# More loads in flight and a new order of all instructions: a recurrent-attention and gated-MLP kernel on one Trainium2 core

## The chip, the cores and the metric

The kernel runs on one core of a Trainium2 chip. The metric is the device time of one execution in microseconds (us), lower is better. A core has five engines that each follow their own instruction queue in order: TensorE (PE, matmuls), VectorE (DVE), ScalarE (ACT), GpSimd (POOL) and SyncE (SP, which here only issues DMAs). They wait for one another and for DMAs by semaphores.

## What is computed

Four arrays q, k, v, alpha of shape (4 batches, 8 heads, 768 steps, 48) go through a gated linear recurrence, and the 3072 x 384 result goes through a two-layer MLP with a smooth gate:

```python
for t in range(S):
    state = alpha[:, :, t, :, None] * state + k_t (outer) v_t      # per batch and head, 48 x 48
    y[:, :, t] = q_t @ state
x = y as (3072 tokens, 384)
h = x @ w_in                                    # 384 -> 2048
g = h * tanh(log1p(exp(h)))
out = g @ w_out                                 # 2048 -> 384, float32
```

The two weights arrive as 64-bit floats and are turned on the chip into a high and a low part of a narrower float each, so that three matmul passes (high x high, high x low, low x high) keep float32 accuracy.

## The kernel before, in words

**Attention.** The 768 steps are cut into 12 pieces of 64, the 4 batches into 2 pairs: 24 chunks, numbered so that chunk n belongs to pair n % 2 and piece n // 2. A chunk loads one tile `qka` (q, k and alpha, 772 KB; chunk 0 in three parts, chunk 1 in two) and one tile `v` (192 KB). DVE makes the running products of alpha by two scans (`scan_rest` L672, `scan_front` L685) and multiplies k and q by them (L681, L695). PE transposes k ("turn", L724), forms the front half (`from_state` L745/L752 and the scores L763), DVE masks the scores (L778, and L583 for chunks taken in pairs), PE forms the back half (L783/L790) and the state's update (L802), and ACT and DVE write the result as a high and a low part into the tile `xs` (ACT `upper` L831, DVE `lower` L837). The state is then added by DVE (L874) or, where the sum was made on PE (L809), copied by ACT (L872). From chunk `PAIR_FROM` = 8 on, two chunks go together.

Four settings say how a chunk does parts of this. In `DIRECT` (chunks below 8 only) PE writes the last two heads straight to their place by extra small matmuls (L745, L783); a chunk not in it writes them to a side tile `x3`, and six small DMAs of 16 KB (`move`, L858), issued by SP or, where `MOVER` says so, by ACT, carry them into `xs`. In `X_PE` PE subtracts the high part in PSUM (`off`, L844) and ACT copies what is left (L852), in place of DVE's `lower`; the state's update then comes after that as a task of its own. In `STATE_PE` PE adds the old state by two more matmuls (L809) and ACT copies the sum, in place of DVE's L874.

**Weights.** There are 16 blocks f. Each is loaded as 64-bit words (768 KB, L415) into one of two `stage` buffers, DVE puts together its bits in three steps (L428, L433, L438), ACT writes the high part (L449), and the low part is the difference, which `W_LOW` gives to DVE (L455), to POOL in two halves (L477), or to PE in two halves (L467, L468, in a named PSUM bank) with an ACT copy after each (L471). A second load of every block from L491 on serves a range check.

**MLP.** A unit is one weight block f on 2 or 4 chunks: nine matmuls into `h_at` ("up", L1017), four ACT steps, one DVE step (L1044), one ACT step (L1051), one DVE step (L1054), and three matmuls for each chunk into `sums_at` ("down", L1089). `SEGMENTS` sets the order of the 100 units: blocks 0 to 3 on chunks 0 and 1, then on chunks 2 and 3; blocks 4 to 10 on chunks 0 to 3; blocks 0 to 9 on chunks 4 to 7; the other blocks on these; then all 16 blocks on chunks 8 to 11, 12 to 15, 16 to 19 and 20 to 23.

**Order.** The order of the instructions on all engines is made at build time by `Plan.order`, a list planner: each task has an engine, a cost, a latency, a key (a due time in units, from `LEAD`, `DUE_SHIFT`, `W_LEAD`, `W_SHIFT`, `Q_LEAD`, `V_LEAD`, `FIRST_W`), needs and buffers; an engine takes the task that can begin earliest, with a penalty `PER_KEY` for each unit of key beyond its first open task. Buffers are 3 for `qka`, 2 for `v`, 2 for `stage`, 2 for `x3`. Before bulk work is there PE gets fills, matmuls whose results are not used (L1165), to keep it running. The planner holds a clock for loads: a load begins `DMA_FIRST` after its issue or when the load before it is through, and takes its size over `DMA_RATE`. A load may be issued only when the loads in flight and itself are within `FLIGHT` kilobytes; the planner sets the load that it has to wait for (`paced`), and this becomes a real wait on SP's queue:

```python
            if t.size:
                room = FLIGHT - t.size
                for x in reversed(loads):
                    room -= x.size
                    if room < 0:
                        at, t.paced = max(at, x.begin + x.late + 0.1), x
                        break
```

SP issues in order, so whatever stands behind a waiting load waits too.

Of the kernel before, what the change touches and what calls it, by code (L numbers as in the profile page):

```python
# [39 lines left out]
QKA = 2 * NSEG * L + NSEG * (L + 1) + 1  # L40
# [10 lines left out]
    "h": 2, "t": 3, "g": 2, "osb": 8,  # L51
}
LAG = 3
LEAD = 5.5
SPREAD = 3.0
W_LEAD = 4.25
GATE = -2.0
Q_LEAD = 4.75
V_LEAD = 9.75
FIRST_W = -22.25  # L60
CHECK_FROM = 105
CHECK_STEP = 2.0
FILLS = 150
# [7 lines left out]
}  # L71
W_SHIFT = {
    0: -30.0, 1: -2.75, 2: -3.75, 3: -1.75, 4: -3.5, 5: -9.25, 6: 0.25, 7: -4.75, 8: 2.5, 9: 2.75,
    10: 2.25, 11: 7.0, 12: -6.25, 13: -7.75, 14: 30.25, 15: -1.75,
}
X_PE = {0, 1}
SIDES = 2
STATE_PE = {2, 6}
PAIR_FROM = 8
BACK_AFTER = 0.8  # L80
DIRECT = {0, 1, 2, 3, 6, 7}
W_LOW = {
    0: ('PE', 'o0'), 1: ('PE', 'o0'), 2: ('PE', 'o3'), 3: ('PE', 'o3'), 4: ('POOL', ''), 5: ('PE', 'o0'),
    6: ('DVE', ''), 7: ('POOL', ''), 8: ('POOL', ''), 9: ('DVE', ''), 10: ('DVE', ''), 11: ('POOL', ''),
    12: ('POOL', ''), 13: ('POOL', ''), 14: ('DVE', ''), 15: ('POOL', ''),
}
MOVER = {
    (1, 1, 0): 'ACT', (1, 2, 0): 'ACT', (1, 2, 64): 'ACT', (2, 1, 0): 'ACT', (2, 2, 64): 'ACT',
    (3, 0, 64): 'ACT', (3, 1, 64): 'ACT', (3, 2, 64): 'ACT', (4, 0, 0): 'ACT', (5, 1, 0): 'ACT',
    (6, 0, 0): 'ACT', (6, 0, 64): 'ACT', (6, 2, 64): 'ACT', (8, 0, 0): 'ACT', (8, 1, 64): 'ACT',  # L90
}
IN_BANK = 0

STOP_AT = 1e9
LOAD_MARGIN = 1.0
LANES = 8
FLIGHT = 1800.0
BLOCK, BLOCK_USED, FETCH_FIRST, FETCH_LAST = 256, 63, 0.8, 2.5
DMA_RATE, DMA_FIRST, DMA_LAST = 285.0, 1.1, 0.9
ENGINES = ("PE", "DVE", "ACT", "POOL", "SP")  # L100
BEGIN = {"PE": 3.0, "DVE": 4.3, "ACT": 2.2, "POOL": 4.2, "SP": 1.2}

# [19 lines left out]
class Plan:  # L122
# [150 lines left out]


KEYS = 60.0
PER_KEY = {'PE': 0.03, 'DVE': 0.02, 'ACT': 0.02, 'POOL': 0.02, 'SP': 0}


COST = {
    "load": (0.45, 2.0), "apart": (0.19, 0.32),  # L280
    "move": (0.63, 2.5), "store": (0.4, 3.0),
    "fill": (0.23, 0.28), "fill0": (0.44, 0.47),
    "off": (0.55, 0.75), "w off": (0.84, 1.08), "lead": (0.47, 0.58), "bits": (0.87, 0.98),
    "w hi": (0.745, 0.88), "w left": (0.42, 0.56), "w lo": (1.05, 1.2), "w lo2": (0.88, 1.0),
    "w check": (0.92, 1.2),
    "scan": (1.16, 1.27), "inverse": (0.09, 0.21), "mult": (0.6, 0.72), "check": (0.2, 0.34),
    "state": (0.48, 0.55), "state0": (0.5, 0.6), "mask": (0.65, 0.8),
    "front": (1.19, 1.32), "front d": (1.59, 1.72), "front0": (0.76, 0.9), "turn": (0.34, 0.6), "turn2": (0.7, 0.95),
    "front2": (2.09, 2.22), "back2": (1.91, 2.04), "back2 last": (1.18, 1.3), "spread": (0.4, 0.4),
    "turned": (0.46, 0.6), "back": (1.14, 1.26), "back1": (0.75, 0.9), "update": (0.7, 0.85),  # L290
    "state on": (0.42, 0.42),
    "x3 hi": (0.16, 0.3), "x3 lo": (0.2, 0.32), "x hi": (0.39, 0.53), "x lo": (0.48, 0.59),
# [17 lines left out]
def fast_path(ctx, tc, qka, v, w, out, good):  # L310
# [65 lines left out]
    add, last_col = plan.add, NSEG * (L + 1)  # L376
# [221 lines left out]
    def chunk(n):  # L598
        nonlocal last_front, v_apart_read, st_apart_read
        b, c = chunks[n]  # L600
        first, last = c == 0, c == NCH - 1
        paired = n >= PAIR_FROM
        st = state[b]
        key = 0.5 * (due[n // 2 * 2] + due[n // 2 * 2 + 1]) + 0.05 * (n % 2) if paired else due[n]
# [858 lines left out]
```

## Time and profile before

| what | us |
|---|---|
| median of 3 runs | 499.11 (498.87 to 499.72) |
| the profiled execution, its own time | 497.71 |
| its span, from the first to the last instruction | 496.0 |
| PE busy | 484.6 (98% of the span) |
| DVE busy | 323.1 (65%) |
| ACT busy | 382.1 (77%) |
| POOL busy | 25.3 (5%) |

The granted TensorE clock is 0.998 over the span, so all durations are at the upper of its two levels, 2.4 GHz. PE's busy time contains the fills. Matmuls are pipelined and their recorded times overlap, so what a burst costs PE is read as the distance from its start to the start of the next burst.

### The profile page before, as it was taken

The page shows a single profiled execution, that of the slowest core. Times are in us where ns is not written, and L with a number is a line of the kernel's source. Part 1 is how long each engine was busy: PE and PEld are TensorE (multiplying, and loading weights), DVE is VectorE, ACT ScalarE, POOL GpSimd, SP SyncE. Part 2 cuts the span into 40 slices and gives each one's busy share as a digit, 9 for nine tenths or more (in the row PEclk, how much of TensorE's full clock was granted, in tenths as well). Part 3 has the DMA queues.
Part 4 walks back from the last instruction along what each step waited for, and adds up shares of the span by engine and source line. Part 5 has one row for each costly group of instructions (what it writes and reads, how often), then busy time and mean ns, then how long its engine had stood idle before and what let it go on. Part 6 is the DMA issues. An engine that isn't in the chain of part 4 may idle for free.

```text
span 496.0 us, 12822 instructions
## 1 busy us (share of the span) xinstructions
PE 484.6 (98%) x5319; PEld 432.5 (87%) x5319; DVE 323.1 (65%) x522; ACT 382.1 (77%) x864; POOL 25.3 (5%) x27
## 2 busy tenths in 40 slices
PE   6999999999999999999999999999999999999995
PEld 4688889899899989999989899999989899999994
DVE  7999999999973694447867783863474343343333
ACT  3578786886788778857777897889789899997772
POOL 2003201413000000000000000000000000000000
PEclk9999999999999999999999999999999999999999
DMA  7877544606000250115152543603153412100001
GB/s 248 316 285 236 181 151 157 238 35 214 13 0 9 78 172 1 66 59 175 28 213 75 183 164 99 207 24 118 71 171 93 172 41 106 64 1 0 1 0 68
DMA packets 18926, 56.22 MB, mean 113 GB/s; under 512 B 3440, under 2 KB 11312, under 8 KB 18864
## 3 DMA queue, kind: packets, MB, share of 16 engines
q1 hardware_dynamic: 18592, 55.11, 32.5%
q8 instruction: 42, 0.69, 0.6%
q10 hardware_dynamic: 272, 0.26, 0.2%
q14 instruction: 20, 0.16, 0.1%
HBM read 48.87 MB, written 4.72 MB: 108 GB/s over the span
## 4 chain that ended last, share of the span: by engine, by line
PE 85%; DVE 9%; DMA 3%; issue 1%; ACT 1%; SPq 0%; DVEq 0%; ACTq 0%
PE sums_at L1089 39%; PE h_at L1017 37%; PE att_at L790 2%; PE att_at L752 2%; DVE w_lead L433 2%; PE h_at L763 2%; DMA ws<-in_wp_dram 1%; DVE w_lead L438 1%; PE att_at L724 1%; DMA qka<-in_qka_dram 1%; PE h_at L802 1%; DVE w_lead L428 1%; DVE t L1044 1%; DVE g L1054 1%; DVE rest L672 1%
## 5 line engine op out<-in xcount | busy, mean ns | idle before, releaser
L1089 PE MATMUL sums_at<-ws,g 128*128 128x384 f32 x1152 | 223.9, 340 | 0.1
L1017 PE MATMUL h_at<-xs,ws 128*128 128x512 f32 (+1 forms) x900 | 214.2, 384 | 0.2 <-DVE t L1044 0.2
L1089 PEld LDWEIGHTS sums_at<-ws,g 128*128 128x128 f32 x1152 | 202.4, 188 | 8.1 <-ACT ws L471 0.4
L1017 PEld LDWEIGHTS h_at<-xs,ws 128*128 128x128 f32 x900 | 163.3, 188 | 28.4 <-DVE t L1044 0.5
L1054 DVE SCALAR_TENSOR_TENSOR g<-t,g 128x512 fp32r<-128x512 f32 (+1 forms) x100 | 67.8, 679 | 124.2 <-ACT g L1051 123.9
L1026 ACT ACTIVATE t<-h_at 128x512 f32<-128x512 f32 (+1 forms) x100 | 58.0, 580 | 63.6 <-PE h_at L1017 60.8
L1051 ACT ACTIVATE g<-t 128x512 fp32r<-128x512 f32 (+1 forms) x100 | 60.3, 604 | 11.5 <-PE sums_at L1089 5.3
L1029 ACT ACTIVATE t<-t 128x512 f32<-128x512 f32 (+1 forms) x100 | 61.3, 613 | 2.3
L1032 ACT ACTIVATE t<-t 128x512 f32<-128x512 f32 (+1 forms) x100 | 61.2, 612 | 2.2
L1044 DVE SCALAR_TENSOR_TENSOR t<-t,h_at 128x512 f32<-128x512 f32 (+1 forms) x87 | 57.1, 657 | 8.3 <-ACT t L1035 8.2
L1035 ACT ACTIVATE t<-t 128x512 f32<-128x512 f32 (+1 forms) x100 | 60.4, 604 | 0.5
L672 DVE TENSOR_TENSOR_SCAN rest<-qka,behind 112x520 f32<-112x520 f32 x24 | 30.4, 1268 | 0.4 <-DMA qka<-in_qka_dram 0.2
L685 DVE TENSOR_TENSOR_SCAN qka<-qka,ahead 112x520 f32<-112x520 f32 x24 | 30.6, 1274 | 0.0
L477 POOL TENSOR_TENSOR ws<-w_lead,ws 128x384 fp32r<-128x384 f32 x14 | 22.1, 1598 | 98.3 <-ACT ws L449 98.3
L1026 ACT ACTIVATION_READ_ACCUMULATOR t<-h_at 128x1 f32 x100 | 19.4, 194 | 0.0
L1041 DVE COPY held<-h_at 128x512 f32<-128x512 f32 x13 | 9.0, 691 | 15.8 <-ACT t L1026 15.8
L831 ACT ACTIVATE xs<-att_at 112x384 fp32r<-112x384 f32 (+1 forms) x24 | 12.2, 513 | 6.2 <-PE att_at L809 3.4
L695 DVE TENSOR_TENSOR qka<-qka 112x512 f32<-112x512 f32 x24 | 16.4, 684 | 0.1
L681 DVE TENSOR_TENSOR qka<-qka,rest 112x512 f32<-112x512 f32 x24 | 15.8, 659 | 0.0
L433 DVE SCALAR_TENSOR_TENSOR w_lead<-ws,w_lead 128x768 int32<-128x768 int32 x16 | 15.7, 982 | 0.1
L438 DVE SCALAR_TENSOR_TENSOR w_lead<-ws,w_lead 128x768 int32<-128x768 int32 x16 | 15.3, 957 | 0.1
L449 ACT ACTIVATE ws<-w_lead 128x768 fp32r<-128x768 f32 x16 | 13.4, 839 | 2.3 <-DVE w_lead L438 2.2
(100 smaller groups left out, 366.7 us busy)
## 6 DMA issues: line engine op xcount, KB each, us to landing
qka<-in_qka_dram SPq DMA_DIRECT2D x22, 772.5 KB, 5.8
ws<-in_wp_dram SPq DMA_DIRECT2D x16, 768.0 KB, 4.5
wc<-in_wp_dram SPq DMA_DIRECT2D x16, 768.0 KB, 4.5
v<-in_vp_dram SPq DMA_DIRECT2D x24, 192.0 KB, 4.5
out_dram<-osb SPq DMA_DIRECT2D x15, 192.0 KB, 2.6
xs<-x SPq DMA_DIRECT2D x104, 16.0 KB, 1.8
out_dram<-part SPq DMA_DIRECT2D x8, 192.0 KB, 2.6
qka<-in_qka_dram SPq DMA_DIRECT2D x2, 260.5 KB, 4.4
```

Source lines behind the costliest of these rows:

```text
L433: nc.vector.scalar_tensor_tensor(lead.tile, words(1), -0x40000000, lead.tile, ALU.bitwise_and, ALU.bitwise_or)
L672: nc.vector.tensor_tensor_scan(t[:, :0:-1], alpha()[:, :0:-1], behind[:, ::-1], 0.0, ALU.mult, ALU.max)
L685: nc.vector.tensor_tensor_scan(a, a, ahead, 0.0, ALU.mult, ALU.max)
L1017: nc.tensor.matmul(p[:, :N].rearrange("p (c t) -> p c t", c=nt), wi[:, z, f, s], x[:, :, s, a], start=m == 0, stop=m == len(passes) - 1,)
L1026: nc.scalar.activation(wide(t), wide(h), AF.Exp, accum_out=vchk[:, at : at + 1])
L1029: nc.scalar.activation(wide(t), wide(t), AF.Square, bias=1.0)
L1032: nc.scalar.activation(wide(t), wide(t), AF.Ln, bias=0.2, scale=0.2)
L1035: nc.scalar.activation(wide(t), wide(t), AF.Exp, scale=-1.0)
L1044: nc.vector.scalar_tensor_tensor(wide(y), wide(t), 2.5, wide(held), ALU.subtract, ALU.mult)
L1051: nc.scalar.activation(g.tile[:, 0, :N], wide(y), AF.Copy, scale=-0.4, accum_out=own)
L1054: nc.vector.scalar_tensor_tensor(g.tile[:, 1, :N], wide(y), -0.4, g.tile[:, 0, :N].bitcast(F32), ALU.mult, ALU.subtract,)
L1089: nc.tensor.matmul(o.tile, g.tile[:, a, j * C : (j + 1) * C], wo[:, z, f], start=begins and m == 0, stop=end and m == 2,)
```

## The change

It raises `FLIGHT` from 1800 to 3500 KB, gives the planner's loads a higher rate (345 for 285), a longer lead-in (1.7 for 1.1 us) and a shorter end (0.6 for 0.9), writes the loads' sizes larger (791 for 692, 263 for 230), and sets the keys and the choices per chunk and block anew, from which the planner makes another order of all instructions. In the choices, chunks 2 and 4 join `X_PE`, chunks 3 and 4 join `STATE_PE` (2 and 6 stay), chunks 0 and 7 leave `DIRECT`; block 3's low part goes from PE to POOL, those of blocks 6, 9 and 14 from DVE to POOL, and those of blocks 8, 11 and 12 from POOL to DVE. No loop, no tile size and no buffer count changes.

```diff
-LEAD = 5.5
+LEAD = 5.75
-W_LEAD = 4.25
+W_LEAD = 5.5
-Q_LEAD = 4.75
-V_LEAD = 9.75
-FIRST_W = -22.25
+Q_LEAD = 4.0
+V_LEAD = 11.5
+FIRST_W = -18.0
 DUE_SHIFT = {
-    0: -3.75, 1: 1.75, 2: 2.5, 3: 1.0, 4: -1.5, 5: 2.0, 6: 2.0, 7: 2.0, 8: -4.5, 9: -6.5, 10: -11.25,
+    0: 2.25, 1: 2.75, 3: -1.5, 4: -1.0, 5: 0.5, 6: -0.75, 7: 1.5, 8: -3.5, 9: -3.5, 10: -14.75,
...
 W_SHIFT = {
-    0: -30.0, 1: -2.75, 2: -3.75, 3: -1.75, 4: -3.5, 5: -9.25, 6: 0.25, 7: -4.75, 8: 2.5, 9: 2.75,
-    10: 2.25, 11: 7.0, 12: -6.25, 13: -7.75, 14: 30.25, 15: -1.75,
+    0: -21.5, 1: -2.0, 2: -1.75, 3: 0.25, 4: -3.25, 5: -8.5, 6: -1.5, 7: -0.75, 8: 2.25, 9: 3.5, 10: 4.5,
+    12: -7.25, 13: 10.25, 14: 26.5, 15: -2.25,
 }
-X_PE = {0, 1}
+X_PE = {0, 1, 2, 4}
-STATE_PE = {2, 6}
+STATE_PE = {2, 3, 4, 6}
-BACK_AFTER = 0.8
-DIRECT = {0, 1, 2, 3, 6, 7}
+BACK_AFTER = 0.25
+DIRECT = {1, 2, 3, 6}
 W_LOW = {
-    0: ('PE', 'o0'), 1: ('PE', 'o0'), 2: ('PE', 'o3'), 3: ('PE', 'o3'), 4: ('POOL', ''), 5: ('PE', 'o0'),
-    6: ('DVE', ''), 7: ('POOL', ''), 8: ('POOL', ''), 9: ('DVE', ''), 10: ('DVE', ''), 11: ('POOL', ''),
-    12: ('POOL', ''), 13: ('POOL', ''), 14: ('DVE', ''), 15: ('POOL', ''),
+    0: ('PE', 'h'), 1: ('PE', 'o2'), 2: ('PE', 'o3'), 3: ('POOL', ''), 4: ('POOL', ''), 5: ('PE', 'o0'),
+    6: ('POOL', ''), 7: ('POOL', ''), 8: ('DVE', ''), 9: ('POOL', ''), 10: ('DVE', ''), 11: ('DVE', ''),
+    12: ('DVE', ''), 13: ('POOL', ''), 14: ('POOL', ''), 15: ('POOL', ''),
 }
 MOVER = {
-    (1, 1, 0): 'ACT', (1, 2, 0): 'ACT', (1, 2, 64): 'ACT', (2, 1, 0): 'ACT', (2, 2, 64): 'ACT',
...
+    (0, 0, 64): 'ACT', (0, 1, 64): 'ACT', (0, 2, 0): 'ACT', (0, 2, 64): 'ACT', (1, 1, 0): 'ACT',
...
-FLIGHT = 1800.0
+FLIGHT = 3500.0
-DMA_RATE, DMA_FIRST, DMA_LAST = 285.0, 1.1, 0.9
+DMA_RATE, DMA_FIRST, DMA_LAST = 345.0, 1.7, 0.6
-PER_KEY = {'PE': 0.03, 'DVE': 0.02, 'ACT': 0.02, 'POOL': 0.02, 'SP': 0}
+PER_KEY = {'PE': 0.01, 'DVE': 0.02, 'ACT': 0.02, 'POOL': 0, 'SP': 0.12}
-                for z, e, early in ((230, (a_at, QKA), 1.0), (460, (0, a_at), 0.0))
+                for z, e, early in ((267, (a_at, QKA), 1.0), (524, (0, a_at), 0.0))
-                "SP", *COST["load"], key - Q_LEAD, load, uses=[q_buf], size=692
+                "SP", *COST["load"], key - Q_LEAD, load, uses=[q_buf], size=791
```

## Rows read from the trace of the kernel before

**Rows 1.** The page, busy time of each engine (share of the span), instructions.
```profile
PE 484.6 (98%) x5319; PEld 432.5 (87%) x5319; DVE 323.1 (65%) x522; ACT 382.1 (77%) x864; POOL 25.3 (5%) x27
```
**Rows 2.** Stretches: us, busy PE, PEld, DVE, ACT, POOL (instructions), clock, DMA share, GB/s.
```profile
10.00:20.00 10.00, 8.85 (x167) 6.35 (x170) 9.68 (x15) 4.88 (x13) 0.00 (x0) 1.00 0.90 319
...
80.00:100.00 20.00, 19.77 (x246) 17.17 (x245) 19.87 (x28) 16.48 (x35) 6.94 (x4) 1.00 0.57 204
100.00:150.00 50.00, 50.00 (x493) 45.32 (x492) 43.91 (x63) 38.33 (x83) 5.01 (x5) 1.00 0.17 59
```
**Rows 3.** PE in order of time: start, us, line, count [idle before and releaser].
```profile
2.85 3.24 PE L1165 MATMUL sums_at<-minus_ident 128*128 128x512 f32 x7 [2.85 <-ACT minus_ident L336]
...
19.57 0.58 PE L783 MATMUL att_at<-probs,v_apart 64*64 64x64 f32 x24
...
22.34 0.60 PE L724 MATMUL att_at<-ident,qka 112*128 112x112 f32 x4
22.72 1.31 PE L1017 MATMUL h_at<-xs,ws 128*128 128x256 f32 x9
...
33.19 0.70 PE L1165 MATMUL sums_at<-minus_ident 128*128 128x512 f32 x2
```
**Rows 4.** Groups and waits of PE: the fills' group, then its last wait but the tail.
```profile
L1165 PE MATMUL sums_at<-minus_ident 128*128 128x512 f32 x31 | 10.5, 466 | 2.8 <-ACT minus_ident L336 2.8
PE h_at L1017 <- DVE t L1044: 0.2, 1, 0.2
```
**Rows 5.** DVE in order of time, 8 to 19 us.
```profile
8.73 0.56 DVE L428 TENSOR_SCALAR w_lead<-ws 128x768 int32<-128x768 int32 x1 [1.12 <-DMA ws<-in_wp_dram]
...
15.24 1.24 DVE L672 TENSOR_TENSOR_SCAN rest<-qka,behind 112x520 f32<-112x520 f32 x1 [0.25 <-DMA qka<-in_qka_dram]
16.40 0.67 DVE L695 TENSOR_TENSOR qka<-qka 112x512 f32<-112x512 f32 x1
...
17.66 1.23 DVE L685 TENSOR_TENSOR_SCAN qka<-qka,ahead 112x520 f32<-112x520 f32 x1
18.81 0.71 DVE L778 COPY_PREDICATED probs<-causal,att_at 128x512 f32<-128x512 uint32 x1
```
**Rows 6.** Waits of SP's DMA queue for loads: us in total, times, longest.
```profile
SPq L415 <- DMA qka<-in_qka_dram: 10.1, 6, 3.5
SPq L646 <- DMA ws<-in_wp_dram: 4.1, 1, 4.1
```
**Rows 7.** One stretch of 1 us in the head; columns as in the stretches above.
```profile
9.00:10.00 1.00, 0.66 (x33) 0.64 (x33) 0.96 (x2) 0.27 (x1) 0.00 (x0) 1.00 0.59 173
```
**Rows 8.** PE in order of time: bursts that the edits add or take away.
```profile
24.77 0.58 PE L745 MATMUL att_at<-qka,v_apart 48*64 48x64 f32 x24
25.17 0.52 PE L752 MATMUL att_at<-qka,state 48*48 48x64 f32 x24
25.51 0.65 PE L763 MATMUL att_at<-qka 48*64 48x64 f32 x32
26.09 0.91 PE L467 MATMUL sums_at<-w_lead,ident 128*128 128x384 f32 x2
...
27.01 0.81 PE L467 MATMUL sums_at<-w_lead,ident 128*128 128x384 f32 x2
...
75.07 0.90 PE L809 MATMUL att_at<-state,ident 112*112 112x192 f32 x4
75.68 2.36 PE L1017 MATMUL h_at<-xs,ws 128*128 128x512 f32 x9
```
**Rows 9.** DVE in order of time: steps that move, and a scan beside POOL.
```profile
31.65 0.55 DVE L837 TENSOR_TENSOR xs<-att_at,xs 128x384 fp32r<-128x384 f32 x1
...
42.66 0.55 DVE L874 TENSOR_TENSOR state<-att_at,state 112x384 f32<-112x384 f32 x1
...
92.12 2.08 DVE L672 TENSOR_TENSOR_SCAN rest<-qka,behind 112x520 f32<-112x520 f32 x1
```
**Rows 10.** The moves into `xs` up to 110 us: from issue to landing.
```profile
DMA to landing us min/median/max: 1.7/2.4/4.6
```

More of the change, by code (lines that the diff above doesn't have):

```diff
@@ L67 @@
 DUE_SHIFT = {
[3 rows of a table removed]
[3 rows of a table added]
 }
 W_SHIFT = {
-    0: -30.0, 1: -2.75, 2: -3.75, 3: -1.75, 4: -3.5, 5: -9.25, 6: 0.25, 7: -4.75, 8: 2.5, 9: 2.75,
-    10: 2.25, 11: 7.0, 12: -6.25, 13: -7.75, 14: 30.25, 15: -1.75,
+    0: -21.5, 1: -2.0, 2: -1.75, 3: 0.25, 4: -3.25, 5: -8.5, 6: -1.5, 7: -0.75, 8: 2.25, 9: 3.5, 10: 4.5,
+    12: -7.25, 13: 10.25, 14: 26.5, 15: -2.25,
 }
-X_PE = {0, 1}
+X_PE = {0, 1, 2, 4}
 SIDES = 2
-STATE_PE = {2, 6}
+STATE_PE = {2, 3, 4, 6}
 PAIR_FROM = 8
-BACK_AFTER = 0.8
-DIRECT = {0, 1, 2, 3, 6, 7}
+BACK_AFTER = 0.25
+DIRECT = {1, 2, 3, 6}
 W_LOW = {
-    0: ('PE', 'o0'), 1: ('PE', 'o0'), 2: ('PE', 'o3'), 3: ('PE', 'o3'), 4: ('POOL', ''), 5: ('PE', 'o0'),
-    6: ('DVE', ''), 7: ('POOL', ''), 8: ('POOL', ''), 9: ('DVE', ''), 10: ('DVE', ''), 11: ('POOL', ''),
-    12: ('POOL', ''), 13: ('POOL', ''), 14: ('DVE', ''), 15: ('POOL', ''),
+    0: ('PE', 'h'), 1: ('PE', 'o2'), 2: ('PE', 'o3'), 3: ('POOL', ''), 4: ('POOL', ''), 5: ('PE', 'o0'),
+    6: ('POOL', ''), 7: ('POOL', ''), 8: ('DVE', ''), 9: ('POOL', ''), 10: ('DVE', ''), 11: ('DVE', ''),
+    12: ('DVE', ''), 13: ('POOL', ''), 14: ('POOL', ''), 15: ('POOL', ''),
 }
 MOVER = {
-    (1, 1, 0): 'ACT', (1, 2, 0): 'ACT', (1, 2, 64): 'ACT', (2, 1, 0): 'ACT', (2, 2, 64): 'ACT',
-    (3, 0, 64): 'ACT', (3, 1, 64): 'ACT', (3, 2, 64): 'ACT', (4, 0, 0): 'ACT', (5, 1, 0): 'ACT',
-    (6, 0, 0): 'ACT', (6, 0, 64): 'ACT', (6, 2, 64): 'ACT', (8, 0, 0): 'ACT', (8, 1, 64): 'ACT',
+    (0, 0, 64): 'ACT', (0, 1, 64): 'ACT', (0, 2, 0): 'ACT', (0, 2, 64): 'ACT', (1, 1, 0): 'ACT',
+    (1, 2, 64): 'ACT', (2, 2, 0): 'ACT', (4, 2, 64): 'ACT', (5, 2, 64): 'ACT', (6, 0, 0): 'ACT',
+    (7, 0, 64): 'ACT', (7, 1, 64): 'ACT', (7, 2, 64): 'ACT', (8, 2, 64): 'ACT', (9, 2, 64): 'ACT',
 }
@@ L288 @@
     "front": (1.19, 1.32), "front d": (1.59, 1.72), "front0": (0.76, 0.9), "turn": (0.34, 0.6), "turn2": (0.7, 0.95),
-    "front2": (2.09, 2.22), "back2": (1.91, 2.04), "back2 last": (1.18, 1.3), "spread": (0.4, 0.4),
+    "front2": (2.107, 2.24), "back2": (1.903, 2.04), "back2 last": (1.18, 1.3), "spread": (0.4, 0.4),
     "turned": (0.46, 0.6), "back": (1.14, 1.26), "back1": (0.75, 0.9), "update": (0.7, 0.85),
@@ L654, in chunk @@
             got_a, got_k, got_q = (
-                add("SP", *COST["load"], -99 + 0.1 * i, load_part(*e), uses=[q_buf], size=230)
+                add("SP", *COST["load"], -99 + 0.1 * i, load_part(*e), uses=[q_buf], size=263)
                 for i, e in enumerate(((a_at, QKA), (k_at, a_at), (0, k_at)))
```

4 rows, old and new, of the table DUE_SHIFT are left out of this document.

## The prediction

> **What bounds the kernel now.** I read the busy times first [rows 1]: PE is busy 98% of the span, and the share says little about where the remaining time is. So I cut the span into stretches [rows 2]: from 100 us on PE never rests while DVE has 6 us free of 50, so there the time is PE's work, and only less work would shorten it. Before that both PE and DVE are full: DVE works 9.68 of 10 us from 10 on, and 19.87 of 20 up to 100. The timeline of PE then shows what "busy" hides in the head [rows 3, 4]. It waits 2.85 us for its first operand, and then runs 31 fills, recorded as 10.5 us. Measuring each of eight stretches of waits and fills from its start to the next real burst (the first runs from 0 to 5.93 us, the last ends at 22.34) gives 14.8 us empty before the first "up" at 22.72. After it there is one more pair of fills at 33.19, some 0.5 us, and one wait of 0.2 us for DVE [rows 3, 4]. So 15.5 us of the span are empty on PE, nearly all in the first 22.7 us, and the change can win there or by taking work off PE.
>
> Who holds the first "up" back? On DVE [rows 5]: the loads keep it waiting 1.12 us before 8.73 and 0.25 us before 15.24. The second chunk's q is multiplied at 16.40, after a scan for the *third* chunk, and its mask starts at 18.81, after the third chunk's second scan. On the DMA side SP's queue waits for earlier loads to land, 10.1 us in one large group and 4.1 us in a single wait near the start [rows 6]; these are the waits that the limit of 1800 KB asks for. They leave holes, as 173 GB/s in the stretch at 9 us beside a mean of 319 over 10 to 20 [rows 2, 7]. So the limit costs transfers, but so far DVE has paid only 0.25 to 1.4 us for it.
>
> **The change part by part.**
>
> *PE's own work.* Block 3's low part leaves PE: two halves, each 27.01 − 26.09 = 0.92 us from start to start [rows 8]: −1.84. Two more chunks add their state on PE, each 75.68 − 75.07 = 0.61: +1.22. Chunks 2 and 4 subtract on PE: two matmuls of 192 columns in chunk 2, which by the same row (two such matmuls, recorded as four) cost 0.61 at most, and by half of it 0.3 at least; in chunk 4 two more of 64 columns. I take 0.35 and 0.5, nearer to the lower end because the operand is the narrower type of the bulk: +0.85, between 0.6 and 1.2. Chunk 7 leaves the direct form: the front half has 24 extra heads, 25.17 − 24.77 = 0.40, in place of 8 of the 24 that follow in 25.51 − 25.17 = 0.34 (0.11): −0.29, and I take the same for the back half: −0.58. Chunk 0's back half saves 0.29 and its subtraction grows by some 0.2; both lie among fills and count nothing. Sum −0.35, with bounds −0.6 to 0.
>
> *DVE's work while it is full.* Chunks 2 and 4 lose `lower`, 0.47 and 0.6 (0.55 each as recorded, the next start some 0.08 earlier; chunk 4 has a small side part too); chunks 3 and 4 lose the addition of the state, 0.47 each: −2.0 [rows 9]. Chunk 7 gains a small side part, +0.2. Block 3's low part on POOL needs no DVE instruction but can stand in its way: a scan that ran beside such a pair took 2.08 us, the same scan elsewhere 1.24 [rows 5, 9], so between 0 and +0.9. Block 6 or 9 moves from DVE to POOL and 8 comes back, about even. Sum between −0.9 and −1.8; I take −1.5.
>
> The Trainium skill, "SBUF — State Buffer", section "Who interferes with whom", says that VectorE and GpSimd share one pair of ports under an exclusive lock, so that the loser is blocked for the whole instruction. The row agrees in kind, with 0.84 us more on one scan; by the rule each of the two halves could block DVE in this way, 1.7 us by an estimate from that row, the DVE sum would be about −0.1, and the time would go towards rival B.
>
> *What moves to ACT.* ACT gets the copies that DVE loses, and chunk 0's four moves; it is busy 4.88 us of 10 at 10 to 20 us and 16.48 of 20 at 80 to 100 [rows 2], so this is hidden. If it is not, each step costs its own half microsecond.
>
> *Loads.* By the new keys the head's queue becomes: chunk 0's three parts, block 0, two v tiles, chunk 1's alpha, block 1 (key 1 − 5.5 − 2 − 4 = −10.5), chunk 1's q and k (−6 − 4 = −10), chunk 2. All fit in 3500 KB as chunk 0 lands, so the wait of 4.1 us [rows 6] goes. Chunk 1's q and k then go out 4 us earlier but behind 768 KB more, 2.4 us at the 319 GB/s of that stretch: a net gain of up to 2 us in a place where DVE did not wait. The 1.12 us before 8.73 stay: the same loads stand ahead of block 0 as now. Later the buffers set a limit of their own: 3 x 772 + 2 x 768 + 2 x 192 = 4.2 MB, and most of them hold data in use. So I give the loads nothing of their own except that the order is free of them.
>
> *The head.* Lower bound of the gain: 0, the order of DVE's work stays as it is. Upper bound: the second chunk's work goes before the third's. Its q could be multiplied at 15.2 in place of 16.4, and its mask could follow the scores at about 16.5 in place of 18.81; everything up to the first "up" is a chain behind that mask (back half at 19.57, "up" 3.15 us later [rows 3]), so 22.72 becomes 20.4: −2.3. This lasts only if DVE keeps up afterwards, and it is full up to 95 us, where PE once waits for it. What keeps it is DVE's relief of 1.5 us, and some slack: the scan at 92 us [rows 9] is the ninth of its line, so chunk 8's, whose x no unit needs before the 37th. I take −1.8, nearer to the upper end because the relief is nearly of that size.
>
> Sum: −1.8 − 0.35 = −2.15. The profiled execution of 497.71 would take 495.55; the median of the runs lies 1.40 above the profiled one, so 497.0.
>
> **The rivals.**
>
> *B, nothing changes.* DVE is full between 8.73 and 95 us and is what PE waits for at 95.7; more loads do not make it faster, and the buffers let few more go. Then only PE's −0.35 stays, partly lost again: 498.9. For it: DVE's waits for loads come to 1.4 us in all [rows 5]. Against it: DVE has less to do.
>
> *C, slower: small moves stand behind large loads.* Chunk 0 now needs six moves before the first "up"; two of them, and most of those of chunks 4, 5 and 7, are issued by SP, on the queue of the loads. The planner gives a move a fixed latency of 2.5 us. Now they take 1.7 to 4.6 us [rows 10], with at most 1.8 MB of loads ahead of them. With 3.5 MB ahead at 319 GB/s [rows 2] it would be 11.0 + 1.7 = 12.7 us. Chunk 0's high and low parts are ready some 7 us before the first "up", so the mechanism decides from about (7 − 1.7) us x 319 GB/s = 1.7 MB in the queue. At the full 3.5 MB the first "up" would come at 28, of which PE could fill about half with attention and low parts: +2.5, less 0.35: 501.2. For it: the queue holds more by design. Against it: four of the six go by ACT, and the buffers, most of them in use by 15 us, bound the queue.
>
> The Trainium skill, "DMA: Bandwidth & Descriptors", section "Queues, rings and completion order", says that a DMA engine takes the descriptors of one queue in the order of the ring and goes round robin between SP's and ACT's queues. By that rule SP's moves wait for all loads ahead and ACT's do not, which makes C's mechanism true for two moves of chunk 0; no row of this trace has a move in a full queue.
>
> *D, much faster.* The head is packed better than I see: chain and relief in full and the 0.54 us of late fills gone: −2.3 − 0.54 − 0.6 − some 1 us of order: 494.7.
>
> **How the numbers follow.** Forecast A 0.48, D 0.10, B 0.20, C 0.22. A measurement of this kernel can tell about 0.2% or 1 us. A and D are faster, B is the same, C is slower: 0.58, 0.20, 0.22. The range goes from 494.6 (D) to 501.0, which leaves out half of C and a little of D.
>
> **What would show it.** First "up" at 20.4 to 22 us in place of 22.72; fills fewer than 31 and shorter by 1.8 us; PE without waits from there to 100 us; one block fewer on L467 and two more bursts on L809; SP's waits for loads nearly gone; DVE still full from 9 to 90 us. C would show as fills before the first "up" with a move's landing as the last event, and moves of 8 us and more. B would show as the same 22.7. I am wrong in kind if PE gets waits beyond 100 us, where I see no cause for any, or if DVE rests between 20 and 90 us.

## The result and the profile after

The changed kernel takes 501.66 us (median of 5 runs, 501.49 to 501.99) where the kernel before took 498.87 beside it (497.39 to 499.72): ratio 1.0064, 95% interval 1.005 to 1.0078. It is slower, by 2.8 us; the prediction said 497.0, with 494.6 to 501.0 as its range. The profiled executions have spans of 496.0 and 499.8 us. Of these 3.8 us, 2.56 are there at the start of the last matmul (490.02 and 492.58). The other 1.2 lie behind it, and 1.0 of them in the last store, which ACT issues. Its rows (KB, median us from issue to landing), before and then after:

```profile
out_dram<-osb ACTq DMA_DIRECT2D x1, 192.0 KB, 3.2
```
```profile
out_dram<-osb ACTq DMA_DIRECT2D x1, 192.0 KB, 4.2
```

This is not a matter of these two executions alone. This section and the next have eighteen traces. Seven come from the kernel before in its own order: there the store lands after 3.2 to 3.3 us, and the last load of instructions (16 KB) is over before it begins. In the other eleven (all of the new order, the two orders made anew, and `before_head2`) that load runs beside the store, which lands after 3.8 to 4.4 us. That the load is the reason is not shown, and how the store landed in the executions without a trace is not on record.

The busy times of the page answer [rows 1], and say as little: PE's share has fallen by one point, but its busy time has risen by 2.5 us with 37 instructions fewer. Whether the loss is work or rest can't be read from it.

```profile
PE 487.1 (97%) x5282; PEld 434.6 (87%) x5282; DVE 319.9 (64%) x513; ACT 384.9 (77%) x867; POOL 23.2 (5%) x29
```

The stretches show where (columns as in [rows 2]). First the kernel after: the head has more transfers, 375 GB/s for 319 between 10 and 20 us, and from 40 to 60 us PE rests 1.09 us.

```profile
10.00:20.00 10.00, 9.06 (x119) 6.44 (x113) 9.97 (x15) 5.31 (x13) 0.00 (x0) 1.00 0.96 375
40.00:60.00 20.00, 18.91 (x292) 16.94 (x291) 19.59 (x31) 14.75 (x43) 6.31 (x4) 1.00 0.53 184
```

The kernel before in the same stretch:

```profile
40.00:60.00 20.00, 19.99 (x300) 18.16 (x298) 19.47 (x37) 16.27 (x46) 7.38 (x4) 1.00 0.55 187
```

PE's waits after (us in total, times, longest), which answer the second line of [rows 4]: the gates of L1044 now hold PE up twice, 1.1 us, and a mask 0.8 us in the head.

```profile
PE h_at L1017 <- DVE t L1044: 1.1, 2, 0.6
PE att_at L790 <- DVE probs L778: 0.8, 1, 0.8
PE sums_at L802 <- DMA v<-in_vp_dram: 0.4, 1, 0.4
PE att_at L724 <- DVE state L874: 0.2, 1, 0.2
```

PE in order of time after (columns as in [rows 3]): the first "up" stands at 23.34 in place of 22.72; the third unit's up (42.00) and the ninth's (58.73, the first one 512 wide) wait for a gate.

```profile
15.07 2.92 PE L1165 MATMUL sums_at<-minus_ident 128*128 128x512 f32 x12
...
19.83 0.58 PE L783 MATMUL att_at<-probs,v_apart 64*64 64x64 f32 x24
...
23.34 1.31 PE L1017 MATMUL h_at<-xs,ws 128*128 128x256 f32 x9
...
42.00 1.30 PE L1017 MATMUL h_at<-xs,ws 128*128 128x256 f32 x9 [0.43 <-DVE t L1044]
...
58.73 2.31 PE L1017 MATMUL h_at<-xs,ws 128*128 128x512 f32 x9 [0.63 <-DVE t L1044]
```

I measured PE from each burst's start to the next burst's start and cut the kernel at units:

```
start of             before   after   after - before
first unit's up       22.72   23.34   +0.62
ninth unit's up       55.32   58.73   +3.41
eighteenth unit's up  99.45  101.94   +2.49
last matmul          490.02  492.58   +2.56

first to ninth unit   32.61   35.38   +2.77
  L1017 (72 matmuls)   9.05    9.68   +0.63   same work: rest
  L1089 (36, 33)       6.88    7.85   +1.54 rest, -0.57 work (0.191 each)
  fills L1165          0.54    1.31   +0.77   rest
  everything else     16.14   16.54   +0.40
```

So the work between the first and the ninth unit is about the same (+0.40 and −0.57), and 2.9 us of rest are new (0.63 + 1.54 + 0.77). Later units give 0.9 us back (fewer attention steps are left there), and from the eighteenth on the distance stays.

Now DVE, after. In the head (this answers [rows 5]) block 1's three steps, L428, L433, L438, stand between the second chunk's scans and its multiplications (16.62, 17.22), and its mask comes at 18.98.

```profile
13.18 0.53 DVE L428 TENSOR_SCALAR w_lead<-ws 128x768 int32<-128x768 int32 x1
...
13.74 0.96 DVE L433 SCALAR_TENSOR_TENSOR w_lead<-ws,w_lead 128x768 int32<-128x768 int32 x1
...
15.77 0.93 DVE L438 SCALAR_TENSOR_TENSOR w_lead<-ws,w_lead 128x768 int32<-128x768 int32 x1
16.62 0.69 DVE L681 TENSOR_TENSOR qka<-qka,rest 112x512 f32<-112x512 f32 x1
17.22 0.69 DVE L695 TENSOR_TENSOR qka<-qka 112x512 f32<-112x512 f32 x1
...
18.98 0.70 DVE L778 COPY_PREDICATED probs<-causal,att_at 128x512 f32<-128x512 uint32 x1
...
38.15 1.77 DVE L433 SCALAR_TENSOR_TENSOR w_lead<-ws,w_lead 128x768 int32<-128x768 int32 x1
...
44.18 2.06 DVE L672 TENSOR_TENSOR_SCAN rest<-qka,behind 112x520 f32<-112x520 f32 x1
...
52.72 1.51 DVE L695 TENSOR_TENSOR qka<-qka 112x512 f32<-112x512 f32 x1
...
54.15 1.38 DVE L700 TENSOR_TENSOR state<-state,rest 112x384 f32<-112x384 f32 x1
```

The last four rows are each some 0.82 us longer than their kind: L433 takes 0.95 elsewhere, L672 1.23, L695 0.69, L700 0.55. POOL after, in order of time, lies beside all four (blocks 3, 4 and 6, two halves each):

```profile
36.55 2.57 POOL L477 TENSOR_TENSOR ws<-w_lead,ws 128x384 fp32r<-128x384 f32 x2 [32.51 <-ACT ws L449]
43.68 3.77 POOL L477 TENSOR_TENSOR ws<-w_lead,ws 128x384 fp32r<-128x384 f32 x2 [4.57 <-ACT ws L449]
52.58 2.54 POOL L477 TENSOR_TENSOR ws<-w_lead,ws 128x384 fp32r<-128x384 f32 x2 [5.13 <-ACT ws L449]
```

With a short one at 37.60 these stretches come to 3.5 us before 60 us. In the kernel before they come to 0.4 there (up to 100 us it is 5.2 after and 2.4 before), as its POOL begins at 45.05, and then it is POOL that waits: the first of its halves takes 4.26 us of the 7.38, while the scan beside it has its usual time.

```profile
45.05 7.38 POOL L477 TENSOR_TENSOR ws<-w_lead,ws 128x384 fp32r<-128x384 f32 x4 [41.03 <-ACT ws L449]
```
```profile
45.66 1.24 DVE L672 TENSOR_TENSOR_SCAN rest<-qka,behind 112x520 f32<-112x520 f32 x1
```

All four stretched steps read two operands from SBUF. The Trainium skill, "SBUF — State Buffer", section "Who interferes with whom", says that this kind of DVE instruction contends with a POOL instruction that reads SBUF, and not with one that only writes it, and that the order of issue decides who blocks; these rows agree on the first and the last, and an experiment below on the second. For the last: each of the four stretched steps began 0.1 to 0.5 us behind a half on POOL, while in the kernel before a DVE step (L433, 44.80) stood ahead of the half at 45.05.

### The profile page after: what moved, and what is told of

Same layout as the page of the kernel before. It is cut to its first block, busy times and chain, and to the rows that moved or that the text cites. A ratio compares the mean times of both kernels' runs of the same rounds, so it can differ in the third digit from the quotient of the medians.

```text
span 499.8 us, 12750 instructions
## 1 busy us (share of the span) xinstructions
PE 487.1 (97%) x5282; PEld 434.6 (87%) x5282; DVE 319.9 (64%) x513; ACT 384.9 (77%) x867; POOL 23.2 (5%) x29
## 4 chain that ended last, share of the span: by engine, by line
PE 86%; DVE 9%; DMA 1%; issue 1%; SPq 0%; ACT 0%; ACTq 0%; DVEq 0%
PE sums_at L1089 40%; PE h_at L1017 37%; PE att_at L790 2%; PE att_at L752 2%; PE h_at L763 1%; DVE w_lead L433 1%; PE att_at L724 1%; DMA ws<-in_wp_dram 1%; DVE w_lead L438 1%; DVE rest L672 1%; PE h_at L802 1%; DVE qka L685 1%; DVE qka L695 1%; DVE w_lead L428 1%; DVE probs L778 1%
## 5 line engine op out<-in xcount | busy, mean ns | idle before, releaser
L1044 DVE SCALAR_TENSOR_TENSOR t<-t,h_at 128x512 f32<-128x512 f32 (+1 forms) x92 | 60.4, 657 | 12.9 <-ACT t L1035 12.6
L672 DVE TENSOR_TENSOR_SCAN rest<-qka,behind 112x520 f32<-112x520 f32 x24 | 30.4, 1268 | 0.4 <-DMA qka<-in_qka_dram 0.3
L685 DVE TENSOR_TENSOR_SCAN qka<-qka,ahead 112x520 f32<-112x520 f32 x24 | 29.6, 1233 | 0.0
L477 POOL TENSOR_TENSOR ws<-w_lead,ws 128x384 fp32r<-128x384 f32 x16 | 20.0, 1269 | 124.7 <-ACT ws L449 124.7
L695 DVE TENSOR_TENSOR qka<-qka 112x512 f32<-112x512 f32 x24 | 18.1, 754 | 0.3 <-DMA qka<-in_qka_dram 0.2
L790 PEld LDWEIGHTS att_at<-probs,v 64*48 64x48 f32 (+1 forms) x736 | 12.9, 126 | 4.1 <-DVE probs L583 1.8
L790 PE MATMUL att_at<-probs,v 64*48 64x64 f32 (+1 forms) x736 | 15.6, 220 | 0.8 <-DVE probs L778 0.8
L438 DVE SCALAR_TENSOR_TENSOR w_lead<-ws,w_lead 128x768 int32<-128x768 int32 x16 | 16.0, 1002 | 0.0
L433 DVE SCALAR_TENSOR_TENSOR w_lead<-ws,w_lead 128x768 int32<-128x768 int32 x16 | 15.9, 999 | 0.1
L681 DVE TENSOR_TENSOR qka<-qka,rest 112x512 f32<-112x512 f32 x24 | 15.6, 651 | 0.0
```

The source lines that it names most:

```text
L672: nc.vector.tensor_tensor_scan(t[:, :0:-1], alpha()[:, :0:-1], behind[:, ::-1], 0.0, ALU.mult, ALU.max)
L685: nc.vector.tensor_tensor_scan(a, a, ahead, 0.0, ALU.mult, ALU.max)
L790: nc.tensor.matmul(y[64 * a : 64 * a + wide, u, j], V()[own, h : h + wide], probs[slot][own, a, j], start=first and j == 0 and not direct ...
L1044: nc.vector.scalar_tensor_tensor(wide(y), wide(t), 2.5, wide(held), ALU.subtract, ALU.mult)
```

## The experiments

Theory P: POOL's subtractions, now three pairs before 60 us, stretch DVE's steps and so the gates. Theory O: the order itself, in which DVE works ahead on weights and scans while PE waits for gates. Beside them stand the prediction's own terms: loads, head, relief of DVE. Ratios are to the kernel before, run beside it, with 95% intervals; "after" alone is 1.0064.

**The loads.** The old order with the waits that 3500 KB ask for, twice, and with no such wait at all:

```diff
     tasks = plan.order()
...
+    for t in tasks:
+        if t.size:
+            t.paced, room = None, 3500.0 - t.size
+            for x in reversed(loads):
+                room -= x.size
+                if room < 0:
+                    t.paced = x
+                    break
+            loads.append(t)
```
```diff
     tasks = plan.order()
+    for t in tasks:
+        t.paced = None
```

> The kernel before in its own order on every engine; only the waits between loads are those of 3500 KB. Theory P: loads land sooner, SP's waits for loads shrink from some 35 us to under 12, but DVE waited only 1.4 us for loads, of which 0.25 us can go: within 0.5 us of the kernel before. Theory L: a deeper queue costs by itself, +1 to +2.5 us. A third view, that the loads hold the head back: 1 us faster or more.

> The kernel before with the waits of 3500 KB and no other change, once more, as the base of the run with the moved head on the same chip. If the 0.15% seen the first time is real: 497.3 to 498.3, ratio 0.997 to 0.9995, first up 22.2 to 22.4. If it was chance: ratio 0.9995 to 1.001.

> The kernel before with no wait for loads in flight at all; only the buffers hold a load back. Rival C (moves and needed loads stand behind large loads): slower than the kernel before, 499.5 to 502, with moves of L858 landing after 8 us or more. If the limit only costs holes in the transfers: as with 3500 KB, 497.2 to 498.3, ratio 0.997 to 0.9995, first up 22.2 to 22.5.

Measured: 0.9985 (0.9971 to 0.9998), 0.998 (0.9968 to 0.9992) and 0.9967 (0.9955 to 0.998; 497.0 us). So more loads in flight are no harm, and by themselves a gain of 0.15 to 0.33%: first up at 22.27, 22.47 and 22.23. The last kernel is the fastest of all here. The moves' landing (us, min/median/max, up to 110 us, as in [rows 10]) in the kernel after, and then with no limit in the old order:

```profile
DMA to landing us min/median/max: 1.7/2.4/5.3
```
```profile
DMA to landing us min/median/max: 1.8/3.1/6.1
```

They grow from 4.6 to 6.1 us at most, not to 12.7. Rival C's time was near the result, its mechanism is not what happened.

The other way round, the new order with the waits of 1800 KB (the first diff with 1800.0):

> The changed kernel in its own order; only the waits between loads are those of 1800 KB. Theory P: the order counts on loads that now come later, so the same to 2 us slower, 501.5 to 503.5. Theory L (the deep queue delays what stands behind it): faster, 499 to 500.5.

Measured: 1.0168 (1.0133 to 1.0203), first up at 26.90: the new order needs its loads early. And the new constants and sizes of the planner's loads with the old keys and choices, ordered anew:

```diff
-FLIGHT = 1800.0
+FLIGHT = 3500.0
...
-DMA_RATE, DMA_FIRST, DMA_LAST = 285.0, 1.1, 0.9
+DMA_RATE, DMA_FIRST, DMA_LAST = 345.0, 1.7, 0.6
...
```

> The kernel before with the new limit of 3500 KB, the new rate, lead-in, end and sizes of loads, order made anew; all keys and choices stay as before. Theory P or O (the loads are not to blame): 496.5 to 498.5, since the same order with the waits of 3500 KB took 497.5. Theory L' (an order made for the new times of loads breaks something): 500 or more.

Measured: 1.0086 (1.0058 to 1.0114), first up at 29.04. The same limit that is harmless in the old order costs 4 us as soon as the planner makes an order from it with keys that were not chosen for it. It is the order that costs here, not the limit. Part of this cost is TensorE's clock: PE rests 1.3 and 1.7 us before 24.61 in this trace, and between 24 and 29 us the granted clock is 0.66 in the mean, so that for a part of this stretch it is at the lower of its two levels. The kernel after with no limit at all was not run.

**POOL.** The low parts that POOL makes are left out, as zeros. First by memsets that wait for nothing:

```diff
-                    nc.gpsimd.tensor_tensor(
-                        lo[:, m], both()[:, m], hi[:, m].bitcast(F32), ALU.subtract
+                    nc.gpsimd.memset(
+                        lo[:, m].bitcast(F32), 0.0
                     )
```

> The changed kernel in its own order, but the 16 halves of low parts on POOL are replaced by memsets of the same places, which read nothing (so the low parts of eight blocks are left out, as zeros). Theory P (POOL and DVE block one another: in the changed kernel's trace DVE instructions that run beside a half on POOL are stretched by some 0.83 us each, 3.5 us in sum before 65 us, against 0.4 us in the kernel before): the stretched instructions go back to their usual length, the first N=512 up comes at 55.5 to 56.5 us in place of 58.7, and the time falls by 2 to 3 us, to about 499. Theory L (the deeper queue of loads, or the order made for it, is what costs): within 0.5 us of the changed kernel, 501.2 to 502.2. Theory W (more work on PE): the same, 501.2 to 502.2.

> The kernel before in its own order, with the 14 halves of low parts on POOL replaced by memsets of the same places (low parts of seven blocks left out, as zeros). Theory P: its DVE instructions are stretched by 0.4 us in sum up to 70 us and by 2.2 us from 74 to 100 us, and PE waits for DVE only once, 0.4 us at 95: 0 to 0.8 us faster, 498.1 to 498.9. Theories L and W: no change.

Measured: 1.005 (1.003 to 1.007) and 0.9998 (0.9984 to 1.0013). Both are spoiled as tests of P: without a wait the memsets all ran in the head, at 3.97 us and on, where PE waited 1.4 us for them and a DVE cast that overlaps them took 2.68 us, though it had begun 1.1 us before the first; in the kernel after it takes 0.88. The three rows are DVE and POOL of this kernel, and then DVE of after:

```profile
2.84 2.68 DVE L333 CAST causal<-causal_f 128x64 uint32<-128x64 f32 x1 [0.59 <-POOL causal_f L328]
```
```profile
3.97 4.44 POOL L477 MEMSET ws<- 128x384 f32 x12
```
```profile
2.80 0.88 DVE L333 CAST causal<-causal_f 128x64 uint32<-128x64 f32 x1 [0.54 <-POOL causal_f L328]
```

So the memsets were made to wait for the high part, as the subtractions do:

```diff
...
+            if t.engine == "POOL" and t.issued is not None:
+                tc.add_manual_dep(
+                    t.issued.ins, t.needs[0].issued.ins.name,
...
```

> As after_noport, but each memset on POOL now waits for the block's high part, as the subtraction did, so that POOL leaves the head of the program alone (in after_noport all 16 memsets ran at 2.8 us and held DVE and PE up by 1.6 us there). Low parts of eight blocks are left out. Theory P, that the blocking of DVE by POOL is the whole loss: 498.2 to 499.2. Theory O, that the order itself costs too (by the first N=512 up DVE has done a scan, a mask and two steps of a weight block more than in the kernel before, some 3 us, while the gates that PE waits for stand behind them): 499.3 to 500.5.

> The kernel before in its own order, the 14 halves on POOL as memsets that wait for their block's high part (low parts of seven blocks left out). Under P and O alike its DVE loses 0.4 us to POOL before 70 us and 2.2 us up to 100 us, and PE waited 0.4 us at 95 us: 0.2 to 0.8 us faster than the kernel before.

Measured: 1.0025 (1.0007 to 1.0043) and 0.9988 (0.9968 to 1.0007). No stretch of over 0.3 us is left before 60 us, though the memsets run within 1 us of the subtractions' places: POOL that only writes did not hold DVE's scans up (two steps of L428 took 0.25 us more beside it). Taking POOL's reads away from the kernel after gives back 0.39 of the 0.64% (the two intervals don't touch), and in the kernel before 0.12%, within its interval nothing. Like with like, with memsets in both, the new order is still 0.37% slower (1.0025 over 0.9988). So POOL accounts for 0.27 to 0.39% of the loss, and either figure is uncertain by 0.2 to 0.3%.

Block 3's low part put back on PE, ordered anew:

```diff
-    0: ('PE', 'h'), 1: ('PE', 'o2'), 2: ('PE', 'o3'), 3: ('POOL', ''), 4: ('POOL', ''), 5: ('PE', 'o0'),
+    0: ('PE', 'h'), 1: ('PE', 'o2'), 2: ('PE', 'o3'), 3: ('PE', 'o3'), 4: ('POOL', ''), 5: ('PE', 'o0'),
```

> The changed kernel with the low part of block 3 back on PE (bank o3, as before), order made anew. Theory P with block 3 as the main culprit (its two halves stretched DVE by 1.0 us at 37 us, and moved what follows): PE gains 1.84 us of work, DVE 1 us or more: 500.5 to 501.5. If only the sum of PE's work counts: 503.5. Theory O: 501 to 503, with PE still waiting for gates at 42 and 58 us.

Measured: 1.0097 (1.0066 to 1.0127). The order made anew still has 2.9 us of stretches before 60 us, and PE waits 2.1 us for gates in it. It can't be read as the price of block 3: again a new order cost more than the edit.

**The gates.** In the order of after, two late gate steps are put forward on DVE, the third past L685 and L837, the seventh past one L433; once alone, once with the waiting memsets:

```diff
...
     tasks = plan.order()
+    for at, over in {2: 2, 6: 3}.items():
+        g = gates[at]
+        here = tasks.index(g)
+        tasks.pop(here)
+        while over and tasks[here - 1] not in g.needs:
+            here -= 1
+            over -= tasks[here].engine == "DVE"
+        tasks.insert(here, g)
```

> The kernel after, with two gate steps of DVE (L1044) put forward in DVE's order and nothing else: the third gate (start 41.98 in the trace of after, 3.22 us behind its ACT step) goes ahead of the scan L685 and of the subtraction L837, some 1.7 us earlier; the seventh (start 58.3, 2.34 us late) goes ahead of one step L433, some 0.9 us earlier. Theory O (the order: DVE works ahead on weights and scans while PE waits for gates, which stood as waits of 1.1 us and as late fills of 0.5 us in the trace of after): 0.5 to 1.3 us shorter than after, ratio to before 1.003 to 1.0055, the ninth unit's first matmul at 57.2 to 58.2 in place of 58.73. Theory P alone (the subtractions on POOL stretch DVE's steps by 3.5 us before 60 us, and that is all): what is put forward only pushes the steps behind it back, 501.3 to 502.0, ratio 1.005 to 1.0065, ninth unit at 58.5 or later.

> The same two gates put forward, and the low parts that POOL makes are written as zeros by a memset that waits for the high part (the low parts of 8 blocks are left out, so the output is not exact): both suspects taken away at once. Theories P and O together: the 0.39% of the stretched steps and the 0.1 to 0.25% of the gates add up, 498.5 to 500.0, ratio 0.9995 to 1.0015. If the gates are worth nothing: as without them, ratio 1.0025. If it stays above 1.003, the two suspects do not carry most of the loss and something else in the order does.

Measured: 1.0067 (1.0048 to 1.0086) and 1.002 (1.0004 to 1.0036). Alone it bought nothing, though in its profiled execution the stretch from second to ninth unit was 1.3 us shorter than in after (27.23 to 58.33 for 26.36 to 58.73). PE in order of time shows where that went by the next turn of k (L724, 65.50 in after). About half went into a gap of PE at 61.80, for which the trace shows no releaser, and half into a later state of L874:

```profile
58.33 2.27 PE L1017 MATMUL h_at<-xs,ws 128*128 128x512 f32 x9
...
61.80 0.47 PE L802 MATMUL att_at<-v,ks 64*48 64x48 f32 x21 [0.41 <-issue]
...
66.44 0.60 PE L724 MATMUL att_at<-ident,qka 112*128 112x112 f32 x4 [0.83 <-DVE state L874]
```

The state is later because of POOL again. With the gate moved, the block's pair of subtractions at 62.26 stretches two DVE steps, where in after (62.57) it stretches the second alone (L681 0.67, L695 1.51 at 62.80). DVE after_gates:

```profile
62.37 1.45 DVE L681 TENSOR_TENSOR qka<-qka,rest 112x512 f32<-112x512 f32 x1
63.75 1.51 DVE L695 TENSOR_TENSOR qka<-qka 112x512 f32<-112x512 f32 x1
```

Together with the memsets the ninth unit starts at 57.06, with no wait; the ratio is that of the memsets alone within the intervals. So theory O in the form "DVE takes the wrong steps first" found no support: with POOL's reads the gain is lost again, and without them there is none to be seen.

**The head.** The move that the prediction credited with 1.8 us, made by hand in the old order with the waits of 3500 KB: the second chunk's multiplication, scores and mask ahead of the third chunk's steps, and four fills out of the closing holes.

```diff
...
+    put(nth("mult_q", 1), nth("scan_rest", 2))
+    put(nth("front_half", 1), nth("inverse", 2))
+    put(nth("mask", 1), nth("inverse", 2))
+    put(nth("check", 2), nth("off", 3))
+    for t in [nth("fill", i) for i in (16, 17, 20, 21)]:
+        tasks.remove(t)
...
```

> The kernel before with the waits of 3500 KB (base: ratios 0.9985 and 0.998) and the move that the prediction credited with 1.8 us, made by hand in its order: the second chunk's multiplication of q (L695) goes ahead of the third chunk's scan L672, its scores and its mask (L778) ahead of the third chunk's L677, L681 and L685; the third chunk's range check on ACT goes behind the copies of the second chunk's result; four fills are taken out of the holes that close. (An earlier attempt put that check ahead of the scan whose result it checks, so that the kernel took its slow general loop; it said nothing on the head.) First up expected at 20.6 to 21.1 in place of 22.27. Theory H (the head is a chain; what the first up gains, the end gains): 1.2 to 1.6 us shorter than the base, ratio 0.9945 to 0.9965. Theory T (DVE's total of work up to some 60 to 90 us is the bound, so that what is put first only puts something else last): the end stays with the base, ratio 0.997 to 0.9995, with new waits or fills of PE of about 1.5 us between 21 and 60 us, the ninth unit's up within 0.4 us of the base's 54.84.

A first form of it, `before_head`, took 17976 us: it put the third chunk's range check ahead of the scan that the check reads, and the kernel took its slow general loop. It says nothing on the head.

Measured: 1.0007 (0.9995 to 1.002); its base had 0.998 and 0.9985, so it is not level but slower by 0.2 to 0.3%. In the traces this is not PE: the last matmul starts at 489.83, in the base's two traces at 489.52 and 489.77. It is the last store, which lands after 4.4 us for 3.3. PE in order of time with the move, and then of the base:

```profile
21.28 1.31 PE L1017 MATMUL h_at<-xs,ws 128*128 128x256 f32 x9
...
24.36 0.58 PE L745 MATMUL att_at<-qka,v_apart 48*64 48x64 f32 x24 [0.38 <-ACT v_apart L739]
...
25.09 0.65 PE L763 MATMUL att_at<-qka 48*64 48x64 f32 x32
```
```profile
22.27 1.32 PE L1017 MATMUL h_at<-xs,ws 128*128 128x256 f32 x9
...
25.07 0.65 PE L763 MATMUL att_at<-qka 48*64 48x64 f32 x32
```

The first up comes 1.0 us earlier and four microseconds later nothing of it is left: the third chunk's scores stand at 25.09 and 25.07, as they need what DVE and ACT have not made sooner. Theory H (what the first up gains, the end gains) is refuted: in this kernel the first up is no mark by which the end moves.

**DVE's relief.** DVE's second step on a weight block, L433, is left out (the signs of these weights are missing, so the result is another): on blocks 1 to 4, before 38 us, in both kernels, and on blocks 5 to 7, between 38 and 58 us, in after. Each time it takes off 3.4 to 3.5 us. In after_less_late the list is (7, 6, 5).

```diff
+    for f in (4, 3, 2, 1):
+        tasks.remove([t for t in tasks if t.emit.__name__ == "signs"][f])
```

> The kernel after, without DVE's second step (L433) on the weight blocks 1 to 4: their signs are left out, so the result is another, and DVE has four steps less, 4 x 0.87 = 3.5 us from start to start, all before 45 us; order, loads and POOL are unchanged. The stretched steps that theory P counts before 60 us come to the same 3.5 us. Theory T (what after lost is DVE's total of time up to about 65 us, whichever step it falls on): the loss of 2.5 us goes, and no more, as PE's own work bounds the rest: 499.0 to 500.0, ratio 1.0 to 1.0025, ninth unit at 55.5 to 57. If DVE's total is not what bounds (a chain of gates, loads or ACT is): less than 1 us shorter, 500.7 to 501.7, ratio above 1.0035.

> The same four steps (L433 of blocks 1 to 4) left out of the kernel before: 3.5 us less for DVE. In the trace of before PE rests only 0.7 us in all after the first up (a pair of fills at 33.19 and a wait of 0.2). Theory T with a balance: DVE and PE end level in before, so relief for DVE buys at most that, 498.0 to 498.9, ratio 0.998 to 1.0; the prediction's relief of 1.5 us was then worth a third of what it was put down for at most. If DVE's work bounds before as well, as the prediction took it: 1.5 us or more shorter, ratio below 0.997.

> The kernel after without DVE's second step (L433) on the weight blocks 5, 6 and 7 (their signs are left out, so the result is another): in its trace these start at 38.15, 48.17 and 57.40 and take 1.70, 0.87 and 0.87 us from start to start, 3.4 us, of which up to 0.8 us of POOL's interference can land on the next step. The same relief on blocks 1 to 4, before 38 us, bought nothing: DVE then waited 3.7 us for PE and ACT, and PE's waits for the gates at 42 and 58.7 us stayed. Theory T2 (what counts is DVE's time between the last such wait at about 38 us and 58 us, where it never rests and PE waits for its gates): 1.2 to 2.4 us shorter than after, ratio 1.0015 to 1.004, the ninth unit's up 56.3 to 57.4 in place of 58.73. If relief there buys nothing either (order alone): less than 0.7 us, ratio above 1.005, the waits for the gates stay.

Measured: 1.0066 (1.0049 to 1.0083), 1.0006 (0.9994 to 1.0018) and 1.0038 (1.0025 to 1.005). Early relief is worth nothing that shows in either kernel, and theory T, DVE's total, fell with it. The trace of after_less shows why. DVE's waits between 10 and 70 us, three of five, which came to 3.7 us where after has one of 0.3:

```profile
DVE probs L778 <- ACT t L1032: 1.3, 1, 1.3
DVE probs L778 <- PE att_at L763: 1.1, 1, 1.1
DVE xs L837 <- ACT xs L831: 0.5, 1, 0.5
```

DVE runs ahead until it needs a score from PE or a step of ACT, and rests. The gate of the ninth unit is then as late as before, relative to PE (PE's row in after_less, then in after_less_late):

```profile
57.72 1.65 PE L1017 MATMUL h_at<-xs,ws 128*128 128x512 f32 x6 [0.65 <-DVE t L1044]
```
```profile
57.63 1.59 PE L1017 MATMUL h_at<-xs,ws 128*128 128x512 f32 x6
```

The profiled execution of after_less was the fastest of its six (500.49, median 501.28), with its first up at 22.57, so its 57.72 is early; from the first up the ninth takes 35.2 us there, in after 35.4, in after_less_late 34.3.

Late relief, where DVE has no rest between 38 and 58 us, takes that wait away and 0.26 of the 0.64% with it (the intervals of 1.0038 and 1.0064 meet at 1.005). That is theory T2 (what counts is DVE's time where gates are late), a little smaller than expected (ninth unit 57.63, where at most 57.4 was expected).

## Why the prediction was wrong

The step that failed is the head's −1.8, the larger of the two terms of the sum, together with the relief of DVE that was to keep it. The first up came 0.62 us later and not 2.3 earlier, and between it and the ninth unit PE got 2.9 us of new rest, as DVE, stretched by POOL, made its gates late.

*What bounds.* "DVE and PE both full up to 95 us" was right as a reading of shares and wrong as a use of them. I took DVE's time anywhere before 95 us for PE's time. before_less and after_less show that 3.5 us of it before 38 us are worth nothing; after_less_late that as much later is worth about 1.3 us where gates are late. In the kernel before PE rests 0.7 us in all after the first up [rows 3, 4]: that was the most that relief could give, and the figure stood in my own first paragraph. (The 31 fills named there include the pair at 33.19; the 14.8 us are right.)

*PE's own work*, −0.35: right in its parts. From start to start over the whole kernel L467 and L468 fell by 1.92 (I had 1.84), L809 rose by 1.35 (1.22), L844 by 1.02 (0.85), the direct form fell by 0.48 (0.58). The sum is about nothing.

*DVE's work while it is full*, −1.5: not a term of the sum, but the ground on which the head was put near its upper end. It failed by size, and its sign turned: −2.1 + 3.1 is +1.0 before the ninth unit. The steps moved away were right, −2.1 before the ninth unit where I had −2.0 in all. But for POOL I counted one pair, 0 to +0.9, took a value near the low end, and put the exchange of blocks 6, 8 and 9 down as even. Every pair counts: blocks 3, 4 and 6 brought 1.0, 0.8 and 1.7 us, 3.5 in place of 0.4, so +3.1. My estimate for a pair of which both halves block, 1.7, is what the third pair cost; my +0.9 is what each of the others cost. Taking the interference away gave back 0.39 of 0.64%.

*What moves to ACT*, nothing: right. Behind the head PE has no wait for ACT in the trace of after, and DVE's waits for ACT up to 100 us come to 1.3 us.

*Loads*, nothing of their own: right, and even a little to the good in the old order. Of SP's waits in [rows 6] the single one of L646 is gone, and L415 waits 0.9 us for loads of qka where it waited 10.1; other waits of SP for loads remain, the longest of 3.7 us.

*The head*, −1.8: failed twice. I worked out what the second chunk would gain by going ahead of the third, which it does (17.22, before the third's scan at 17.83). But block 1's three steps went ahead of both, so that the first up came at 23.34 and not at 20.4. A due time moved in the list doesn't tell the order on an engine, and I did not look for what else could be put there. And the chain of "first up earlier, so end earlier" does not hold: before_head2 had the earlier first up, and its last matmul came no earlier.

*Rivals.* B, nothing changes, had the head right, where PE gains nothing, but no loss. C gave 501.2 by a mechanism that the landings exclude. That the time would be longer because DVE is held up while gates are due was written down only as a bound of one term, not as a rival of its own: the rule of the Trainium skill, "SBUF — State Buffer", section "Who interferes with whom", stood beside it; the trace of after bears it out, with 0.8 to 1.7 us for each pair, and counted for three pairs it leads past B.

*The marks.* Two bursts more on L809, fewer on L467, SP's waits fewer, DVE full: seen. Fills fewer than 31: 32 are there. First up at 20.4 to 22: it is 23.34. PE without waits up to 100 us: it waits 1.1 us for gates.

*The end*: the prediction had no term for it. The last store lands 1.0 us later in the profiled execution.

What stays open: with the memsets and the moved gates 0.2% remains (after_gates_memset, 1.002, interval 1.0004 to 1.0036). In the profiled execution of that kernel the last matmul stands at 490.46, 0.4 us behind before, and the last store takes 4.2 us for 3.2, so most of what remains there lies in the store. What makes it land later, and the rest of PE's loss, no run separates.

## What to carry to other kernels

When two engines are both full, relief of the one is worth only what the other waits for it, in that stretch: read the waits, not the shares, and ask for each relieved step who waits for it and when. A start that comes earlier is worth nothing until the next thing that the chain needs comes earlier too, so follow it for two or three steps before counting it. And before work is given to a lightly used engine, list every instruction of the full engine that will run beside it: POOL, at 5% of the span, cost DVE 3.1 us more where 2.1 had been taken off it. Look at the end of the span too: one us of the loss stood behind the last matmul.

## What was not expected of the hardware

A subtraction of 128x384 on POOL, 1.0 us by itself, makes one DVE step with two SBUF operands 0.82 us longer, nearly the same for a scan, a multiplication and an integer step; begun just behind a DVE step, the POOL half took 4.26 us in place of 1.0 and DVE lost nothing. Memsets on POOL left the same DVE steps alone, but a small cast on DVE that overlaps them took 2.68 us in place of 0.88. The gate at 46.48, which reads one operand from PSUM, kept its 0.41 us beside POOL. The last store of 192 KB landed after 3.8 to 4.4 us in the eleven traces where a load of instructions runs beside it, and after 3.2 to 3.3 us in the seven where none does.
